# Banded attention before an MLP: from 128-row tiles turned by TensorE to 32x32 blocks turned by VectorE

## The chip, the cores and the metric

The kernel runs on one core of one Trainium2 chip. The metric is the device time of one execution in microseconds, and lower is better. Before the change three runs gave 407.55 us as the median, with 404.62 and 410.42 us as the ends.

## The reference

Eight batches of eight heads, 576 positions, head width 64. A query sees the keys within 32 positions on either side; eight global positions see everything and are seen by all. The attention result goes, token by token, through a two-layer MLP with softplus.

```python
scores = scale * np.matmul(q, k.transpose(0, 1, 3, 2))          # q, k, v: 8 x 8 x 576 x 64
mask = np.abs(pos[:, None] - pos[None, :]) <= window            # window = 32
mask = mask | is_global[:, None] | is_global[None, :]           # 8 global positions
scores = np.where(mask, scores, -1000000000.0)
attn = np.exp(scores - np.max(scores, axis=-1, keepdims=True))
attn = attn / (np.sum(attn, axis=-1, keepdims=True) + 1e-09)
x = np.matmul(attn, v) ...                                       # 4608 tokens x 512
h = x @ w_in                                                     # 512 -> 2048
g = np.maximum(h, 0.0) + np.log1p(np.exp(-np.abs(h)))
return g @ w_out                                                 # 2048 -> 512
```

## The kernel before

**The MLP.** The 4608 tokens are cut into nine tiles of 512. For each tile `first` (L770) makes 16 chunks of 128 hidden features with four matmuls each, `soft` (L776) applies softplus on ScalarE, and `second` (L781) makes four blocks of 128 tokens with 16 matmuls each, accumulated in one bank. `oev` copies a finished block out of PSUM and SyncE's queue writes it to memory. The first tile's `first` is done in two halves of 256 columns. Per tile this is 64 + 64 matmuls over 512 columns, in all kernels of this document.

**The attention of one unit.** A unit is 64 query positions of one batch, all eight heads, taken as four pairs of heads; there are 72 units, eight to a tile. `sc` (L632): for each pair of heads one matmul with the queries of both heads as 128 stationary columns (the query tile `qx` holds zeros in the other head's half) against 136 key columns: 128 positions around the unit and the eight global keys, which are stored among the others. `top` (L638), on VectorE, adds the mask and keeps the row extreme. `ex` (L659), on ScalarE, four exponentials with the row's own bias. `su` (L667 to L669): row sums and reciprocals on VectorE. `no` and `gc` (L675, L679), on GpSimd, multiply by the reciprocal. `tp` (L685): four 128x128 transposes by matmul, and `pt` copies them back from PSUM. `val` (L728, L735) takes four units: value matmuls over 64 columns, two column halves of the array at a time. The global queries' own rows are handled once a batch (`sg`, `mx`, `gexp`, `gsum`, `tg`, `lge`, `ov`, `oze`) and are laid into the result by a further small matmul group (`rt`, L728).

**The preparation of one batch.** GpSimd's queue loads q and k and casts them to bf16 on the way (`load_qk`, L233) into one buffer each, `qn` and `kn`. As there is one buffer, the load of the next batch waits until the transposes of this one are done. `pick` (L474) takes the global rows out by 64 small matmuls; `tk` and `tq` (L516, L524) turn k and q with 128 transposes by matmul, and `kev` and `qev` copy them out of PSUM. v is loaded by SyncE's queue, cast by GpSimd (L446), and copied a second time shifted by 64 rows (`shift`, two DMAs).

**What sets the order.** Each piece of work is a job with a cost written by hand for each engine that may do it. `_Order.run` lays all jobs out in time before the program is emitted and so fixes the order on every engine's queue and which engine does the copies. An engine works through its queue in that order: a job that is late holds up everything behind it. `KINDS` says how many of the eight PSUM banks a kind of job may hold, and `SLOTS` how many buffers there are. `gate` makes the exponentials of one tile wait until the softplus of the tile before is through, so that ScalarE changes its table twice a tile. `AHEAD` says how many units of the next tile are done early.

Of the kernel before, what the change touches and what calls it, by code (L numbers as in the profile page):

```python
# [18 lines left out]
class _Order:  # L19
# [17 lines left out]
    def add(self, cost, emit, deps=(), rank=5, opens=(), uses=(), table=None, moves=0, array=128):  # L37

        job = dict(cost=cost, emit=emit, deps=[d for d in deps if d is not None], rank=rank, opens=list(opens),
                   table=table, moves=moves, array=array, n=len(self.jobs), at=None, end=None)  # L40
# [13 lines left out]
    def room(self, opens):  # L54
# [3 lines left out]
        spare = 0  # L58
        for pool, key in opens:
            cap = self.slots.get(pool) or self.kinds[pool][0]  # L60
# [16 lines left out]
    def run(self, free):  # L77
# [13 lines left out]
        while ready:  # L91
            best = None
            for j in ready:
# [3 lines left out]
                if j["opens"]:  # L97
                    t = self.room(j["opens"])
                    if t is None:
                        continue  # L100
                    t0 = max(t0, t)
                for e in j["cost"]:
# [51 lines left out]
def kernel(  # L154
# [20 lines left out]
    G = 64  # L175
    NJ = S // G
    NT5 = (S + P - 1) // P
    NH5 = 2 * NT5
    HP = H // 2
    W = G + NG  # L180
    EXT = P + NG
    KD = d_model // P
    KF = d_ff // P
    NN = B * NJ
    NU = NN // 4
    assert d_model == H * D and D == 64 and S == 576 and NG == 8 and H == 8 and n_tokens == NN * G
# [6 lines left out]
    SUMMED = 9  # L193
    HALVED = 1
    W_IN = 1
    W_OUT = 4
    QK1 = 2
    AHEAD = [1, 2, 3, 3, 3, 3, 3, 3]

    TILES = [2] * (NU // 2)  # L200
    assert sum(TILES) == NU

# [3 lines left out]
    sets = ctx.enter_context(tc.tile_pool(name="setup", bufs=1))  # L206
# [4 lines left out]
    def temp(shape, dt, name):  # L211
        return sets.tile(shape, dt, tag=name, name=name)


    SRC = (q, k, v)
    QR = 8
    NQ = S // QR
    stage = ctx.enter_context(tc.tile_pool(name="stage", bufs=NT5))
    PS = {}

    def load_v(b, t):
        st = PS["in", b, 2, t] = stage.tile([P, H * D], FP32, tag="v", name="v")
        lo, hi = max(0, t * P - WIN), min(S, (t + 1) * P - WIN)
        p0 = lo - (t * P - WIN)
        nc.sync.dma_start(out=st[p0:p0 + hi - lo, :].rearrange("p (h d) -> p h d", h=H),
                          in_=SRC[2][b, :, lo:hi, :].rearrange("h s d -> s h d"))


    qn = const([P, H, QR * D], BF16, "qn")
    kn = const([P, H, QR * D], BF16, "kn")  # L230

    def load_qk(b, which, h0=0, h1=H):
        nc.gpsimd.dma_start(out=(qn, kn)[which][0:NQ, h0:h1, :],  # L233
                            in_=SRC[which][b, h0:h1].rearrange("h (q r) d -> q h (r d)", r=QR))

    load_qk(0, 1, 0, H // 2)
    vA = [const([P, NT5, H * D], BF16, f"vA{i}") for i in range(2)]
    vB = [const([P, NT5 - 1, H * D], BF16, f"vB{i}") for i in range(2)]

    gi = const([P, 2 * NG], I32, "gi")  # L240
    nc.sync.dma_start(out=gi[:, :], in_=global_idx.rearrange("(one n) -> one n", one=1).bitcast(I32)
                      .to_broadcast([P, 2 * NG]))

    load_qk(0, 0, 0, H // 2)
    ident = temp([P, P], FP32, "ident")
    make_identity(nc, ident[:])
    ident_b = const([P, P], BF16, "ident_b")
    nc.vector.tensor_copy(ident_b[:], ident[:])
# [4 lines left out]
    def clear(eng, ap):  # L253
        names = "abcd"[:len(ap.shape) - 1]
        flat = ap.rearrange("p " + " ".join(names) + " -> p (" + " ".join(names) + ")") if len(names) > 1 else ap
        eng.memset(flat.bitcast(I32), 0)

    gf = const([P, NG], FP32, "gf")
    nc.vector.tensor_copy(gf[:], gi[:, 0:2 * NG:2])
    posA = temp([P, NT5], FP32, "posA")  # L260
# [23 lines left out]
    def blank_q(i, eng):  # L284
# [3 lines left out]
        for p in range(HP):  # L288
            for h in range(2):
                eng.memset(qx[i][h * D:(h + 1) * D, p, :, 1 - h, :].bitcast(I32), 0)  # L290
# [658 lines left out]
```

## Time and profile before

| what | us |
|---|---|
| runs: lowest, median, highest | 404.62, 407.55, 410.42 |
| span of the profiled execution | 409.3 |
| VectorE, ScalarE, GpSimd busy in it | 247.2, 293.2, 149.8 |
| first MLP matmul starts | 38.56 |
| last piece of the chain, a copy of the last block, starts | 405.64 |

A row of the profile names the line, the engine, what is written and read, the count, the busy time, and the mean length of one instruction. The lengths of matmuls overlap, so the pace of a series is read from the starts in the timeline, not from the mean. "PEclk" is the clock granted to TensorE, 1.00 being full.

### The profile page before, as it was taken

To read this page: it belongs to the slowest core of one execution; us is meant where nothing else is said; L and a number is where in the kernel's file an instruction comes from. 1 tells how busy PE (TensorE), PEld (TensorE's weight loads), DVE (VectorE), ACT (ScalarE), POOL (GpSimd) and SP (SyncE) were. 2 spreads that over 40 slices of the span, in tenths; PEclk is the share of its full clock that TensorE was granted. 3 is DMA by queue.
4 is the path that set the end of the run, shared out by engine and by line. 5 is a ranking of instruction groups with operands and counts; after the bars stand their busy time and mean duration, and the time that the engine had idled before them with its cause. 6 is when DMAs were issued, how large, how long until landed. Compare 5 with 4: busy or idle time off the path is not lost.

```text
span 409.3 us, 11475 instructions
## 1 busy us (share of the span) xinstructions
PE 364.0 (89%) x4401; PEld 213.6 (52%) x4448; DVE 247.2 (60%) x1084; ACT 293.2 (72%) x736; POOL 149.8 (37%) x268
## 2 busy tenths in 40 slices
PE   2747999987999769998999799977999999999996
PEld 2525885653556345654565445634465455545442
DVE  5598758994598515874597429852587577334011
ACT  4486979884799628984898459951998698694720
POOL 8988133760078001840184005800183045023000
PEclk9999999999999969999999979996999999999999
DMA  6699968788021940159116911294012011001012
GB/s 97 138 194 198 202 136 163 171 183 129 0 74 41 179 99 27 54 97 188 55 54 98 176 38 51 46 193 101 27 54 80 0 54 54 0 27 53 0 54 77
DMA packets 61031, 37.47 MB, mean 92 GB/s; under 512 B 42032, under 2 KB 55344, under 8 KB 60976
## 3 DMA queue, kind: packets, MB, share of 16 engines
q0 software_dynamic: 16800, 13.65, 22.7%
q1 hardware_dynamic: 44176, 23.08, 21.7%
q8 instruction: 35, 0.57, 0.6%
q14 instruction: 20, 0.16, 0.1%
HBM read 36.71 MB, written 9.44 MB: 113 GB/s over the span
## 4 chain that ended last, share of the span: by engine, by line
PE 56%; DMA 18%; DVE 9%; POOL 8%; issue 4%; ACT 4%; POOLq 0%; DVEq 0%; ACTq 0%
PE o L781 23%; PE h L770 19%; DMA qn<-in_q_dram 18%; PE tp L685 3%; PE pick L474 2%; PE s L632 2%; DVE sm L667 2%; DVE st L638 2%; POOL vA L446 2%; DVE rs L669 2%; ACT pe L659 1%; PE xo L728 1%; POOL qx L290 1%; POOL pn L675 1%; PE xo L735 1%
## 5 line engine op out<-in xcount | busy, mean ns | idle before, releaser
L675 POOL TENSOR_TENSOR pn<-pe,rs 128x512 bf16<-128x512 f32 x72 | 74.9, 1041 | 202.9 <-DVE rs L669 191.5
L770 PE MATMUL h<-xT,win 128*128 128x512 bf16 (+1 forms) x620 | 141.8, 368 | 1.7 <-issue 0.7
L781 PE MATMUL o<-wout,g 128*128 128x512 bf16 x549 | 132.4, 379 | 1.5 <-issue 0.6
L776 ACT ACTIVATE g<-h 128x512 bf16<-128x512 f32 (+1 forms) x160 | 85.5, 558 | 47.8 <-PE h L770 45.2
L638 DVE CUSTOM_DVE_ANT_0 st<-s,mask 128x136 f32<-128x136 f32 x288 | 69.8, 296 | 55.5 <-PE s L632 52.8
L659 ACT ACTIVATE pe<-st,nb 128x136 f32<-128x136 f32 x288 | 93.9, 408 | 3.2 <-DVE nb L638 3.2
L770 PEld LDWEIGHTS <-win 128*128 128x128 bf16 x640 | 60.7, 100 | 50.3 <-issue 5.4
L781 PEld LDWEIGHTS <-g 128*128 128x128 bf16 x576 | 53.2, 98 | 51.4
L667 DVE TENSOR_REDUCE sm<-pe 128x4 f32<-128x544 f32 x63 | 44.9, 713 | 9.1 <-ACT pe L659 8.8
L685 PE MATMUL tp<-ident_b,pn 128*128 128x128 bf16 x288 | 28.9, 229 | 8.7 <-POOL pn L675 5.9
L632 PE MATMUL s<-kx,qx 128*128 128x136 bf16 x288 | 34.0, 239 | 0.3 <-issue 0.2
L632 PEld LDWEIGHTS <-qx 128*128 128x128 bf16 x288 | 24.6, 105 | 17.4 <-issue 4.6
L446 POOL CAST vA<-v 128x512 bf16<-128x512 f32 (+3 forms) x48 | 28.4, 611 | 13.4 <-DMA v<-in_v_dram 12.2
L685 PEld LDWEIGHTS <-pn 128*128 128x128 bf16 x288 | 19.9, 101 | 21.5 <-POOL pn L675 16.9
L419 ACT COPY qx<-tq 64x576 bf16<-64x576 bf16 x42 | 26.8, 637 | 4.5 <-PE tq L524 3.9
L419 DVE COPY osb<-o 128x512 f32<-128x512 f32 x18 | 12.4, 687 | 28.6 <-PE o L781 28.6
L638 DVE DVE_READ_ACCUMULATOR2_ANT nb<- 128x1 f32 x288 | 24.0, 83 | 0.0
L419 ACT COPY pt<-tp 128x512 bf16<-128x512 bf16 x34 | 19.9, 586 | 4.0 <-PE tp L685 3.8
L669 DVE TENSOR_SCALAR rs<-rs,notg 128x4 f32<-128x4 f32 x72 | 20.1, 280 | 2.7 <-DVE rs L668 0.2
L516 PE MATMUL tk<-ident_b,kn 72*64 72x72 bf16 x512 | 14.5, 206 | 8.2 <-DMA kn<-in_k_dram 8.2
L474 PE MATMUL pick<-qn,pick 72*32 72x128 bf16 x256 | 6.7, 265 | 16.7 <-DMA qn<-in_q_dram 16.4
L419 DVE COPY qx<-tq 64x576 bf16<-64x576 bf16 x22 | 16.6, 752 | 6.6 <-PE tq L524 6.4
(110 smaller groups left out, 423.0 us busy)
## 6 DMA issues: line engine op xcount, KB each, us to landing
out_dram<-osb SPq DMA_DIRECT2D x36, 256.0 KB, 2.0
v<-in_v_dram SPq DMA_DIRECT2D x24, 256.0 KB, 7.9
vB<-vA SPq DMA_DIRECT2D x16, 256.0 KB, 3.7
kn<-in_k_dram POOLq DMA_DIRECT2D x7, 576.0 KB, 9.7
qn<-in_q_dram POOLq DMA_DIRECT2D x7, 576.0 KB, 14.4
v<-in_v_dram SPq DMA_DIRECT2D x16, 192.0 KB, 4.6
win<-in_moe_w_in_dram POOLq DMA_DIRECT2D x4, 512.0 KB, 10.8
wout<-in_moe_w_out_dram POOLq DMA_DIRECT2D x4, 512.0 KB, 11.5
```

The costliest lines, as they stand in the source:

```text
L419: (nc.scalar.copy if e == "ACT" else nc.vector.tensor_copy)(out, in_)
L446: nc.gpsimd.tensor_copy(to[r], at[r])
L632: nc.tensor.matmul(out=ps[:, y, :], lhsT=qx[i][:, x * 2 + y, j, :, :].rearrange("c h q -> c (h q)"), rhs=kf[:, x * 2 + y, j * W:j * W + EX ...
L638: nc.vector.tensor_tensor_reduce(out=PS["st", n][:, p, :], in0=PS["s", n, x][:, y, :], in1=mask[:, j, :], scale=-SCALE, scalar=3.0e38, op0 ...
L659: nc.scalar.activation(out=pe[:, p, 0:EXT], in_=PS["st", n][:, p, :], func=AF.Exp, bias=PS["nb", n][:, p:p + 1], scale=-1.0, **({"accum_ou ...
L667: nc.vector.reduce_sum(out=sm[:], in_=PS["pe", n][:, :, 0:EXT], axis=AX)
L669: nc.vector.tensor_scalar(out=rs[:], in0=rs[:], scalar1=notg[:, j:j + 1], scalar2=None, op0=OP.mult)
L675: nc.gpsimd.tensor_tensor(out=pn[:].rearrange("c p (a s) -> c p a s", a=2), in0=wide[:, :, :, 0:G], in1=rs[:].unsqueeze(2).unsqueeze(3).to ...
L685: nc.tensor.transpose(out=ps[:, p, :], in_=PS["pn", n][:, p, :], identity=ident_b[:])
L770: nc.tensor.matmul(out=h[:, :], lhsT=w_in_t[c // 4][:, kd, c % 4 * P:(c % 4 + 1) * P], rhs=PS["xT", m][:, kd, lo:hi], start=(kd == 0), sto ...
L776: nc.scalar.activation(out=PS["g", m, c][:, lo:hi], in_=PS[key][:, :], func=AF.Softplus)
L781: nc.tensor.matmul(out=PS["o", m, ns][:, :], lhsT=PS["g", m, kf][:, ns * P:(ns + 1) * P], rhs=w_out_t[kf // 4][:, kf % 4, :], start=(kf == ...
```

## The change

The attention is rewritten; the MLP and the scheduler's principle stay. A "pair" n is now 128 query positions (four blocks of 32), all eight heads, so there are 36, four to a tile. The four quarters of the partitions hold heads: quarter r holds heads 2r and 2r+1, with the head width split in two halves (`w`) of 32.

- **Loads.** SyncE's queue loads q, k and v in fp32 into three staging buffers (for the first batch ScalarE's queue shares q and k). `add_cast` casts them to bf16 on GpSimd or ScalarE, two halves each; q and k are stored so that two neighbouring positions form a 4-byte pair. The load of the next batch waits for this cast only. The shifted copy of v is gone.
- **Turning.** `turn` transposes 32x32 blocks of such 4-byte pairs on VectorE, from SBUF to SBUF. The global key rows are written as one block of 32 columns between the others (`fill`), so a block's scores are four neighbouring blocks: previous, own, next, global.
- **Scores.** `sc`: for each block, half and head one matmul of a 32x32 tile over 128 columns, 64 in all for a pair; the two heads of a quarter go to different column quarters. For the first four pairs the mask is added by 32 more matmuls against an identity, and the exponentials are as before. For the others VectorE adds the mask (`ma`), takes the maximum over 1024 columns (`mx`), GpSimd subtracts it (`sub`), ScalarE does one exponential over 1024 columns (`ex`), VectorE sums (`su`), GpSimd multiplies and writes bf16 pairs (`no`), and VectorE turns them (`tp`).
- **Values.** `val` takes the four pairs of a tile (two in the first tile) in one job: for each two blocks four or five steps of eight matmuls on 32x64 tiles over 32 or 64 columns, which write four banks at once. The job is marked `urgent`: while it could start but lacks banks, the scheduler places nothing else that opens one. `vg` holds the finished rows of the global queries' own results in the place of the global block of values, so no separate group lays them in.
- **Global rows.** `sg` holds four banks; 48 matmuls. `mx`, `gexp`, `tpg` (a turn on VectorE), `ov` (144 matmuls on 32-row tiles over 64 columns), `gv`. `pick` has 72 matmuls for q and 72 for k, each over 128 columns.
- **Scheduler.** `KINDS` no longer asks for spare banks, `AHEAD` is one pair from the third tile on, and `room` counts several openings of one pool by one job.

```diff
-    KINDS = dict(h=(3, 1), o=(2, 1), s=(2, 1), pick=(1, 2), gt=(1, 1), tk=(2, 2), tq=(2, 2), sg=(2, 1), tg=(1, 0), ov=(1, 0),
-                 tp=(3, 0), rt=(1, 0), xo=(2, 0))
+    KINDS = dict(h=(3, 0), o=(2, 0), s=(4, 0), pick=(1, 0), sg=(4, 0), ov=(1, 0), xo=(4, 0))
...
+            first = []
+            for j in ready:
+                if j["urgent"]:
+                    t = self.room(j["opens"])
+                    first.append((j, max(d["end"] + self.HOP for d in j["deps"]), 1e9 if t is None else t))
...
+                    if any(pool in self.kinds for pool, key in j["opens"]) and any(
+                            u is not j and due <= t0 < free_at for u, due, free_at in first):
+                        continue
...
+    def load_qk(eng, b, w, rs):
+        for r in rs:
+            eng.dma_start(out=stage[w][quad(r), :, :, :].rearrange("i c e d -> i c (e d)"),
+                          in_=SRC[w][b, 2 * r:2 * r + 2].rearrange("h (c i e) d -> i (h c) (e d)", i=BL, e=2))
...
+        def turn(e, w):
+            if w == 0:
+                x = qb[:].rearrange("p c d e -> p c (d e)").bitcast(I32).rearrange("p (h c) (w i) -> p h c w i", h=2, w=2)
+                y = qx[i][:].bitcast(I32).rearrange("p h w (c i) -> p h c w i", i=BL)
+                V.transpose(out=y, in_=x)
+                return
...
+        def pck(e, w):
...
+            for c in range(NC):
+                for x in range(2):
+                    for r in range(R):
+                        nc.tensor.matmul(out=ps[quad(r), :, :], lhsT=pick[quad(r), c, x, g0:g0 + BL],
+                                         rhs=(qb, kb)[w][quad(r), :, :, x].rearrange("p (h c) d -> p h c d", h=2)[:, :, c, :],
+                                         start=(c == 0 and x == 0), stop=(c == NC - 1 and x == 1))
...
+            for x, (b, j) in enumerate(bl):
+                e0 = first_slot(j)
+                for w in range(2 + masked):
                     for h in range(2):
+                        for r in range(R):
+                            nc.tensor.matmul(out=PS["s", n, h][quad(col_of(r, h)), x, :],
+                                             lhsT=qx[b % 2][quad(r), h, w, j * BL:(j + 1) * BL] if w < 2 else eye[quad(r), :],
+                                             rhs=kx[b % 2][quad(r), h, w, e0 * BL:(e0 + SL) * BL] if w < 2 else
+                                             mask[quad(r), j, :, :].rearrange("p s i -> p (s i)"),
+                                             start=(w == 0), stop=(w == 1 + masked))
+
+        def ma(e, h):
+            V.tensor_tensor(out=PS["st", n][:, h, :, :], in0=PS["s", n, h][:, :, :],
+                            in1=mask[:, j0:j0 + PB, :, :].rearrange("p j s i -> p j (s i)"), op=OP.add)
...
+            V.reduce_max(out=m[:], in_=PS["s", n, h0][:] if masked else flat(PS["st", n], h0, h1), axis=AX)
...
+            nc.gpsimd.tensor_tensor(out=t, in0=t, in1=over(PS["m", n, y][:], SL * BL), op=OP.subtract)
...
+                nc.scalar.activation(out=t, in_=t, func=AF.Exp, scale=SCALE)
...
+                V.reduce_sum(out=sm[:], in_=flat(PS["st", n], h0, h1), axis=AX)
...
+            V.transpose(out=f[0], in_=f[1])
...
+                    steps = [(None, 0, 2, GLOB[a], GLOB[z])]
+                    if j > 0:
+                        steps.append((j - 1, 0, 1, PREV[a], None))
+                    steps.append((j, 0, 2, SELF[a], PREV[z]))
+                    steps.append((j + 1, 0, 2, NEXT[a], SELF[z]))
+                    if j + 2 < NJ:
+                        steps.append((j + 2, 1, 1, NEXT[z], None))
+                    for t, (key, x0, nx, s0, s1) in enumerate(steps):
+                        for h in range(2):
+                            for c in range(R):
+                                r = col_of(c, h)
+                                nc.tensor.matmul(
+                                    out=PS["xo", v_, r][h * D:(h + 1) * D, c0 + x0 * BL:c0 + (x0 + nx) * BL],
+                                    lhsT=vg[i][quad(c), h, :] if key is None else vb[i][quad(c), h, key, :],
+                                    rhs=near_by(n, c, h, x + x0, s0, s1),
+                                    start=(t == 0), stop=(t == len(steps) - 1))
```

## The prediction

> **What bounds the kernel now.** I read the busy shares first, then the spans in stretches of about one tile, then the chain of waits and the timeline of TensorE. The shares:
>
> ```profile
> PE 364.0 (89%) x4401; PEld 213.6 (52%) x4448; DVE 247.2 (60%) x1084; ACT 293.2 (72%) x736; POOL 149.8 (37%) x268
> ```
>
> TensorE leads, but a share says nothing of a stage. The stretches (span, busy time and count for PE, PEld, DVE, ACT, POOL, then granted clock, DMA share, GB/s) do:
>
> ```profile
> 80.00:120.00 40.00, 35.55 (x452) 20.34 (x456) 28.31 (x129) 30.02 (x71) 13.54 (x22) 1.00 0.47 94
> 120.00:165.00 45.00, 38.95 (x492) 22.25 (x498) 25.38 (x112) 31.09 (x76) 12.41 (x21) 0.92 0.43 84
> ...
> 300.00:345.00 45.00, 44.63 (x536) 25.23 (x542) 32.27 (x132) 38.16 (x94) 18.74 (x32) 1.00 0.13 43
> 345.00:390.00 45.00, 44.63 (x313) 22.82 (x316) 14.30 (x62) 32.02 (x63) 6.19 (x10) 1.00 0.07 24
> ```
>
> Late on, where nothing is loaded, TensorE is busy for 44.63 of 45 us: it is the bound. Where batches are loaded it idles 4 to 6 us and the clock falls to 0.92. The chain says why, with the timeline at one such place:
>
> ```profile
> 131.10 15.02 DMA qn<-in_q_dram
> 146.17 1.90 PE pick L474 x64
> ...
> 354.22 6.04 PE h L770 x28
> ...
> 398.10 7.52 PE o L781 x34
> ```
>
> ```profile
> 101.85 0.63 PE L474 MATMUL pick<-qn,pick 72*32 72x128 bf16 x32 [2.69 <-DMA qn<-in_q_dram]
> 102.31 0.62 PE L474 MATMUL pick<-kn,pick 72*32 72x128 bf16 x32
> 102.86 0.29 PE L632 MATMUL s<-kx,qx 128*128 128x136 bf16 x2
> ...
> 251.71 0.20 PE L735 MATMUL xo<-pt,vA 128*64 128x64 bf16 x2
> 251.74 0.20 PE L735 MATMUL xo<-pt,vB 128*64 128x64 bf16 x2
> 251.87 0.84 PE L685 MATMUL tp<-ident_b,pn 128*128 128x128 bf16 x8
> ```
>
> `pick` stands in TensorE's queue behind a q load of 15 us; the same 64 matmuls take 1.01 us (101.85 to 102.86) after a short wait, 1.90 us after a long one. The waits list puts 16.4 us on this load. Idle time of all stretches from 37 to 390 us adds to 22.8 us.
>
> Split of the time after the first MLP matmul: 405.6 − 38.6 = 367 us. The MLP is 1088 matmuls of 512 columns at 0.216 us (6.04/28) = 235 and 128 of 256 columns at half of that = 14, in all 249. Idle is 23. So 95 us are attention on TensorE, changes of its tile form among them.
>
> **TensorE after the change, in pieces.** Counted from the diff: scores 36·64 + 4·32 = 2432 matmuls over 128 columns; values 43 steps × 8 × 8 batches = 2752 over mostly 64; `pick` 1152 over 128; `sg` 384 over 288 in the mean; `ov` 1152 over 64. Together 7872, against some 3200 now.
>
> What one costs is the open question, since no row shows 32-row tiles. `pick` runs four column tiles at once: 1.01 us / 64 = 15.8 ns each, 63 ns a group. The value rows run two at once: a group each 30 to 32 ns (251.71, 251.74). So a group of concurrent tiles takes its columns' time plus little, however many are in it.
> - If eight tiles run at once in scores, `sg` and values (two heads in each of four quarters) and four in `pick` and `ov`: 2432/8 × 0.056 = 17, 2752/8 × 0.032 = 11, 1152 × 0.0158 = 18, 384/8 × 0.123 = 6, 1152/4 × 0.032 = 9. Sum 61 us.
> - If never more than four run at once, as `pick` shows: 38 + 22 + 18 + 12 + 9 = 99 us.
>
> I take 61: the tiles of a group share neither stationary place nor bank, and nothing in the rows shows a group growing with its members. The upper bound stays in the range. Moving operands with a step of two elements (`pick`, values) have no row either; if they halved the pace, values and `pick` would cost 29 us more.
>
> [...]
>
> Changes of tile form: from the last value group (251.74) to the next work is 0.13 us where groups follow each other every 0.03, so 0.1 us is lost. 78 groups of small tiles, most between 128-row work: 12 us.
>
> TensorE in all: 249 + 61 + 12 = 322, of which some 8 us (first batch's `pick`, `sg`, `ov`, first scores and values) lie before the first MLP matmul. 314 remain.
>
> **The loads.** q and k move from GpSimd's queue to SyncE's, and wait for a cast, not for TensorE. The next batch is asked for about a tile (36 us) ahead; a load took 15 us. So the 16.4 us of waits and the slow `pick` after them go; I charge nothing, since ahead of the load stands only a cast. SyncE's queue now has four q, four k and eight v issues a batch (five v issues took 6.80 us at 84.43), and the output writes queue behind them; an output block is due each 3.5 us and has two buffers, so an issue series of up to 7 us might cost about 2 us a batch. This is inside the stall term below. The shifted copy of v within SBUF (16 DMAs) disappears, off the path.
>
> **VectorE, per tile, by rows of before.** Mask add, 8 × 0.69 (the 128x512 cast out of PSUM took 689 ns) = 5.5; maximum and sum over 1024, each 713/544 × 1024 = 1.34 us, eight = 10.7, reciprocals 0.7; turns `tp`, for which no row exists: 512 words lie between 0.42 (bf16 copy of 512) and 0.69, I take 0.69, 2.8. Per batch: `turn` 2 × 1152 words at the same pace 2.7, `mxg` 2.4 (524 ns for 352 columns, 381 for 224), `tpg` 0.7, small ones 1.9: 7.7 × 8/9 = 6.8. Half the copies out of PSUM 2.8. Sum 29.3 us, against 247.2/9 = 27.5 now. If the turns ran at half pace, 5.5 us more.
>
> **The others, per tile.** ScalarE: exponentials fall from eight units of 1.63 us (408 ns × 4) to four of about 1.1, transposes' copies go, casts come: 25 us against 32.6. GpSimd: subtract and multiply at 2 × 1.04 = 2.08 us each, eight = 16.6, plus three of six casts at about 1.4: 21 against 16.6. All below TensorE's 314/9 = 35.
>
> **In order, does the exponential phase fit?** From the last softplus: table 1.3, `gexp` 2.8, first exponential 1.1, sum 1.5, three GpSimd multiplies 6.2, turn 0.7, values 1.4, copy 0.7: about 16 us. Beside it TensorE has 64 `second` matmuls (13.8 us), `sg`, `ov`, `pick`, later scores: 18 us. It fits, with little to spare.
>
> **Start and end.** Now the first scores start at 18.35 and the first MLP matmul at 38.56. After: k and q come 12 to 13 us after start, cast and turn 2.7, first scores near 16; two pairs' scores 1.7, sixteen exponentials of 0.39 = 6.3, `gexp` 3, multiply, turn, values (half clock) and copy 4: 31 us. The end (last copy and write) stays 3.7 us.
>
> **Stalls.** Idle without the load was 22.8 − 16.4 = 6.4 us over eight tiles; with a tighter phase I take double a tile, 9 × 1.7 = 15.
>
> Sum: 31 + 314 + 15 + 3.7 = 364 us against the profiled 409.3; the median of the runs is 1.75 us lower than that, so 362.
>
> **Rivals.**
> 1. *The queue cannot feed the small tiles.* If 15.8 ns a matmul, the least that any row shows, is a floor: 7872 × 0.0158 = 124, 63 more than the sum: 425 us. For: no row shows less. Against: both rows there are as fast as their columns allow, so neither shows the queue's own limit. Chance 0.15. [...]
> 2. *VectorE becomes the bound (the slower side).* A pair leaves VectorE after `mx` for `sub`, and after `su` for `no`, and VectorE's queue is fixed. If it stands through both multiplies of 2.08 us of each pair, a tile takes 29.3 + 16.6 = 46 us: 31 + 8 × 46 + 27.6 (last MLP) + 4 = 431. It decides once over 7 of those 16.6 us are uncovered, as a tile on TensorE takes 36.6 with stalls. For: VectorE now has steps before, between and after GpSimd's; for half-pace turns less is needed. Against: six score buffers let two pairs run ahead. Chance 0.20.
> 3. *Banks.* `sg` and `val` each want four of eight banks at once, 17 times, and while a due `val` waits nothing else opens one. One `second` block holds its bank 16 × 0.216 = 3.5 us; with 2.5 us lost each time: 362 + 43 = 405, no change. Chance 0.10.
>
> **How the numbers follow.** Forecast 0.55, the rivals 0.45. The likeliest case alone: 345 (no stalls, start at 29) to 399 (never more than four tiles at once, 38 more). The range must reach the rivals at 405, 425 and 431, and their uncertain sizes: 345 to 440, leaving out about 0.15. About 2% is what a measurement of this kernel can tell from no change, so faster is under 399, slower over 416: faster 0.55, same 0.10, slower 0.35.
>
> **What would show it.** The sum holds if no wait on a q or k load is left, first MLP work starts near 31 us, MLP matmuls keep 0.216 us, and scores take about 0.5 us a pair. Rival 1: scores of a pair take 1 us and values of a tile over 4. Rival 2: VectorE busy over 80% in the stretches with TensorE waiting on `tp`. Rival 3: gaps before `val` or `sg` ended by PSUM copies. Wrong altogether would be a GpSimd step far over 2.08 us: strided writes have no row here.

## The result and the profile after

The changed kernel takes 471.66 us as the median of four runs (466.70 to 473.27); the kernel before took 406.09 beside it (403.46 to 410.42). The ratio is 1.159, with a 95% interval from 1.149 to 1.168. The forecast of 362 us had the wrong sign, and its range ended at 440. The profiled execution has a span of 469.3 us. Ratios and their intervals, here and below, leave out the few slow executions of a kernel; medians are of all of them.

From the page after the change: the span, the busy shares, the granted clock in 40 slices, the queue that brings instructions (packets, MB, share), and the chain that ended last.

```profile
span 469.3 us, 19736 instructions
...
PE 362.0 (77%) x9038; PEld 206.2 (44%) x9088; DVE 247.3 (53%) x448; ACT 220.7 (47%) x410; POOL 173.2 (37%) x136
...
PEclk9955559996899979995999799979978999998899
...
q8 instruction: 71, 1.16, 1.1%
...
PE 74%; issue 16%; SPq 5%; DMA 3%; POOL 1%; DVE 1%; ACT 0%; ACTq 0%; POOLq 0%
```

No other engine has become the bound: all are below TensorE's share, and VectorE, ScalarE and GpSimd together hold 2% of the chain. TensorE itself went from 89% to 77% busy in a longer span, so it stands more. "issue" in the chain, time in which the engine waited for nothing that the profile shows, is 16%. The waits for q loads, 18% of the chain before, are gone: DMA is 3% of it. The line of q8 counts 71 packets of instructions; the page of the kernel before has half as many:

```profile
q8 instruction: 35, 0.57, 0.6%
```

The weight loads, one for each matmul, rose in the same proportion, from 4448 to 9088.

The same stretches as before (busy time and count by engine, granted clock, DMA share, GB/s), and one of the start:

```profile
0.00:57.00 57.00, 17.87 (x945) 15.28 (x946) 32.84 (x88) 21.63 (x84) 24.73 (x51) 0.72 1.14 200
80.00:120.00 40.00, 30.65 (x892) 20.80 (x896) 24.67 (x45) 24.24 (x42) 18.36 (x11) 0.87 0.64 139
120.00:165.00 45.00, 39.75 (x1311) 23.47 (x1324) 31.46 (x55) 24.14 (x38) 24.34 (x14) 0.99 0.65 143
300.00:345.00 45.00, 36.93 (x873) 19.87 (x878) 25.12 (x43) 20.36 (x34) 15.85 (x9) 0.89 0.19 52
345.00:390.00 45.00, 39.68 (x821) 20.32 (x826) 24.52 (x42) 20.35 (x34) 16.30 (x9) 0.92 0.07 26
```

From 300 to 390 us, where hardly anything is loaded and TensorE was busy for 44.63 of 45 us before, it now stands for 5 to 8 us in each stretch, at a clock of 0.89 to 0.92. The waits (engine, line, what was waited for: total, times, longest) say that it waits for "issue", most of all ahead of the small tiles, and ahead of MLP matmuls (L806) that come after such a series:

```profile
PEld L770 <- issue: 32.6, 20, 4.7
...
PE xo L770 <- issue: 28.0, 12, 4.6
...
PEld L622 <- issue: 24.8, 29, 4.2
...
PE s L622 <- issue: 19.1, 13, 4.0
...
POOL vb L414 <- DMA stage<-in_v_dram: 16.2, 1, 16.2
...
PE o L806 <- issue: 11.4, 22, 3.2
```

The timeline of TensorE at one tile's values shows the form of these stops (start, length, instructions of a row; in brackets the idle time ahead of it):

```profile
299.57 3.83 PE L806 MATMUL o<-wout,g 128*128 128x512 bf16 x17 [1.81 <-issue]
303.32 0.24 PE L770 MATMUL xo<-pt,vg 32*64 32x64 bf16 x8
303.38 0.44 PE L770 MATMUL xo<-pt,vb 32*64 32x32 bf16 x32
303.63 0.27 PE L770 MATMUL xo<-pt,vg 32*64 32x64 bf16 x8
...
305.26 0.25 PE L770 MATMUL xo<-pt,vb 32*64 32x32 bf16 x7
307.81 0.37 PE L770 MATMUL xo<-pt,vb 32*64 32x32 bf16 x25 [2.31 <-issue]
307.98 0.28 PE L770 MATMUL xo<-pt,vg 32*64 32x64 bf16 x8
308.08 0.49 PE L770 MATMUL xo<-pt,vb 32*64 32x32 bf16 x32
308.50 1.05 PE L622 MATMUL s<-kx,qx 32*32 32x128 bf16 x63
311.82 0.26 PE L622 MATMUL s<-kx,qx 32*32 32x128 bf16 x1 [2.27 <-issue]
```

TensorE stops in the middle of a series: seven of 32 equal matmuls run, then nothing for 2.31 us, then the other 25; the profile shows no operand that they wait for. Between the two stops stand 25 + 8 + 32 + 63 = 128 matmuls, each with its weight load: 256 instructions. A packet on q8 has 16 KB (1.16 MB in 71). All 9088 weight loads are in the trace. Counted through by 128, the first matmul behind a stop of over 0.7 us that ended on "issue" has a load with a number from 91 to 96, in 34 of 35 stops: nearly all lie at the same place modulo 256.

The packets themselves are in the trace's DMA records. The next table is worked out from them, for some stops: when TensorE stood, when the packet of the next block started and how long it took, from the packet's start to the first instruction, from the beginning of the block before to the packet's start, and the busy share of the DMA engines in the 4 us ahead of the packet (over 1: packets overlap in an engine).

```
stood             packet         to first   after block   DMA busy
                  start + took   instr.     began         before
25.62 -  30.75    28.15 + 0.92   2.60       4.14          1.22
32.91 -  37.22    34.31 + 1.33   2.91       3.56          1.22
45.81 -  50.04    47.70 + 0.95   2.34       4.12          1.20
110.92 - 113.56   111.03 + 1.06  2.53       1.20          0.66
213.45 - 216.59   214.25 + 0.97  2.34       2.21          0.70
252.59 - 254.11   251.51 + 1.28  2.60       1.13          0.01
309.24 - 311.82   309.33 + 1.16  2.49       1.51          0.51
431.15 - 433.86   431.30 + 1.19  2.57       1.18          0.00
```

So this is how it went in this execution. In 16 stops the block before began behind a stop itself, so that its beginning is seen exactly. In each of them the packet for the next block started only after the present block had been entered: 1.1 to 1.2 us later with idle DMA engines (busy share below 0.3, six stops), 1.2 to 2.2 us at shares of 0.5 to 0.7 (four), and 3.2 to 4.1 us later in five of the six with full ones (shares of 1.10 to 1.24; 1.9 in the other). The packet takes about 1 us (0.9 to 1.3 in the table), and its first instruction runs 2.2 to 2.9 us after its start, once 3.4. Such blocks come 3.4 to 3.7 us apart with idle DMA engines, in the start 6.4 to 6.7 (24.0 to 50.0 us). An MLP matmul takes 0.216 us, so a block of them lasts 27.6 us, longer than any of these distances; a block of small tiles at 8 ns lasts 1.0 us, and TensorE stands for the rest. No supply further ahead than one block shows in these stops.

The long stops also lower the granted clock (experiment 8, which fills those within the values, has it at 0.50 for 32.0 us behind the first MLP matmul, for 76.4 here). In the clock records of this execution, which begin at 21.2 us, it is 1.00 or 0.50. In the start it is 0.50 for 44.4 us (24.6 to 68.9). Later, but for the last one at the end, each stretch at 0.50 begins within or less than 1 us behind a stop of over 2 us, and is 3.4, 6.8 or 10.2 us long (for instance 307.9 to 314.7, behind the stop that ended at 307.81). Not every such stop is followed by one: 384.76 to 387.23 us is not.

Where the time went, by the starts of TensorE's matmuls: the time from one start to the next is booked on the first of the two, or as standing where it is over 0.7 us (us; "with filling" is an experiment below; standing ahead of the first MLP matmul is in the first row).

| | before | after | doubled | halved | joined (6) | with filling |
|---|---|---|---|---|---|---|
| up to the first MLP matmul | 38.6 | 57.0 | 69.9 | 53.7 | 53.3 | 62.2 |
| MLP matmuls | 252.0 | 259.5 | 269.8 | 261.6 | 254.3 | 252.0 |
| other matmuls | 92.5 | 84.1 | 113.5 | 61.2 | 82.7 | 87.5 |
| filling | | | | | | 42.9 |
| standing over 0.7 us | 22.1 | 64.5 | 110.0 | 39.2 | 52.2 | 38.6 |
| from the last matmul's start to the end | 4.1 | 4.3 | 4.3 | 4.2 | 4.3 | 4.2 |
| span | 409.3 | 469.3 | 567.4 | 420.0 | 446.8 | 487.4 |

The 60.0 us between the two kernels are 42.4 of standing, 18.4 of a later start and 7.5 of MLP, mostly at half clock, less 8.4 that the attention gained. Of the 64.5 us of standing, 62.9 in 29 of 31 stops ended on "issue"; of the 22.1 before, 2.5 did, and 17.6 ended with a q load. Behind the first MLP matmul the clock is at 0.50 for 76.4 us, before for 23.9.

### The profile page after: what moved, and what is told of

Its sections match the earlier page's. It is cut to its first block, busy times and chain, and to the rows that moved or that the text cites. A ratio compares the mean times of both kernels' runs of the same rounds, so it can differ in the third digit from the quotient of the medians.

```text
span 469.3 us, 19736 instructions
## 1 busy us (share of the span) xinstructions
PE 362.0 (77%) x9038; PEld 206.2 (44%) x9088; DVE 247.3 (53%) x448; ACT 220.7 (47%) x410; POOL 173.2 (37%) x136
## 3 DMA queue, kind: packets, MB, share of 16 engines
q8 instruction: 71, 1.16, 1.1%
## 4 chain that ended last, share of the span: by engine, by line
PE 74%; issue 16%; SPq 5%; DMA 3%; POOL 1%; DVE 1%; ACT 0%; ACTq 0%; POOLq 0%
PE o L806 28%; PE h L795 27%; PE xo L770 6%; PE s L622 5%; PE pick L495 4%; DMA stage<-in_k_dram 3%; PE ov L585 3%; SPq L241 2%; SPq L246 2%; PE sg L548 1%; POOL kb L414 1%; DVE xT L414 0%; ACT kb L414 0%; ACT g L801 0%; DVE osb L414 0%
## 5 line engine op out<-in xcount | busy, mean ns | idle before, releaser
L806 PE MATMUL o<-wout,g 128*128 128x512 bf16 x544 | 133.5, 398 | 11.9 <-issue 11.4
L676 POOL TENSOR_TENSOR pn<-st,rs 128x1024 bf16<-128x1024 f32 (+1 forms) x40 | 69.4, 1743 | 131.9 <-DVE rs L669 120.0
L806 PEld LDWEIGHTS <-g 128*128 128x128 bf16 x576 | 56.3, 101 | 80.7 <-issue 22.8
L647 POOL TENSOR_TENSOR st<-st,m 128x1024 f32<-128x1024 f32 x32 | 60.5, 1896 | 81.5 <-DVE m L639 81.5
L629 DVE TENSOR_TENSOR st<-s,mask 128x512 f32<-128x512 f32 x64 | 41.8, 675 | 11.5 <-PE s L622 11.3
L622 PE MATMUL s<-kx,qx 32*32 32x128 bf16 x2304 | 33.9, 248 | 15.6 <-issue 15.1
L667 DVE TENSOR_REDUCE sm<-st 128x8 f32<-128x1024 f32 x32 | 38.2, 1193 | 13.6 <-ACT st L660 13.6
L770 PE MATMUL xo<-pt,vb 32*64 32x64 bf16 (+1 forms) x2176 | 26.7, 210 | 23.5 <-issue 23.5
L639 DVE TENSOR_REDUCE m<-st 128x8 f32<-128x1024 f32 x32 | 38.6, 1206 | 0.2
L622 PEld LDWEIGHTS <-qx 32*32 32x32 bf16 x2304 | 26.2, 98 | 20.9 <-issue 20.6
L770 PEld LDWEIGHTS <-vb 32*64 32x64 bf16 x2176 | 24.4, 110 | 24.7 <-issue 24.5
L495 PEld LDWEIGHTS <-pick 32*32 32x32 bf16 x1152 | 20.2, 101 | 30.1 <-issue 11.8
L660 ACT ACTIVATE st<-st 128x1024 f32<-128x1024 f32 x32 | 32.1, 1054 | 0.1
L686 DVE STREAM_TRANSPOSE pt<-pn 128x512 int32<-128x512 int32 (+1 forms) x40 | 25.5, 639 | 5.0 <-POOL pn L676 5.0
L414 ACT COPY osb<-o 128x512 f32<-128x512 f32 x11 | 6.4, 582 | 45.7 <-PE o L806 27.6
```

What stands on the lines that cost most here:

```text
L414: {"ACT": nc.scalar.copy, "DVE": V.tensor_copy, "POOL": nc.gpsimd.tensor_copy}[e](out, in_)
L495: nc.tensor.matmul(out=ps[quad(r), :, :], lhsT=pick[quad(r), c, x, g0:g0 + BL], rhs=(qb, kb)[w][quad(r), :, :, x].rearrange("p (h c) d -> ...
L622: nc.tensor.matmul(out=PS["s", n, h][quad(col_of(r, h)), x, :], lhsT=qx[b % 2][quad(r), h, w, j * BL:(j + 1) * BL] if w < 2 else eye[quad( ...
L629: V.tensor_tensor(out=PS["st", n][:, h, :, :], in0=PS["s", n, h][:, :, :], in1=mask[:, j0:j0 + PB, :, :].rearrange("p j s i -> p j (s i)") ...
L639: V.reduce_max(out=m[:], in_=PS["s", n, h0][:] if masked else flat(PS["st", n], h0, h1), axis=AX)
L647: nc.gpsimd.tensor_tensor(out=t, in0=t, in1=over(PS["m", n, y][:], SL * BL), op=OP.subtract)
```

## The experiments

The theory: TensorE's instructions come in blocks of 256, and a stretch that uses one up faster than the next can come stands still. The rivals: small tiles cost their columns and the stops belong to other engines; each small matmul has a floor; the loads or the late v set the start. All kernels here are the changed one with the edit shown, or kernel 6 with it where that is said.

**1. More instructions, same columns.** Besides the scores below, the two-block steps of `val` and the steps of `ov` behind the first are cut in two in the same way.

```diff
-                            nc.tensor.matmul(out=PS["s", n, h][quad(col_of(r, h)), x, :],
...
+                            for z in range(1 + (w == 1)):
+                                zn = SL * BL // (1 + (w == 1))
+                                zs = slice(z * zn, (z + 1) * zn)
+                                nc.tensor.matmul(out=PS["s", n, h][quad(col_of(r, h)), x, zs],
...
```

> The same result and the same columns in the same order, with 3392 matmuls more: the second half of d in the scores goes as two matmuls of 64 columns, the two-block steps of the values as two of 32, the sums over V of the global rows as two of 32. Theory (instructions come to TensorE in blocks of 256, and a block takes about 3.4 us to come): 6784 instructions more are 26.5 blocks more, most of them inside bursts; worked out from the order of the instructions with 3.4 us a block, the pauses grow by 65 us, so 530 to 565 us, pauses still every 256 instructions, 97 instruction packets for 71. Rival A (a small tile costs its columns, the pauses belong to waits on other engines): 471 to 478 us. Rival B (a floor for each small matmul, 15 ns or so, eight tiles at once): 3392 x 15 ns = 51 us, about 520, but with no pauses at multiples of 256.

Measured 569.62 us, ratio to before 1.403 (1.386 to 1.421). The page of this kernel, queue and chain:

```profile
q8 instruction: 97, 1.59, 1.2%
...
PE 71%; issue 25%; DVE 3%; POOL 0%; DVEq 0%; POOLq 0%
```

The same sums cost 98 us more, 4.6 us above the theory's range. Standing behind the first MLP matmul grew by 45 us, and 54 of the 56 stops that ended on "issue" lie at the same place modulo 256 (loads 91 to 96 of 128) though there are now 97 blocks. That excludes rival A. A price per matmul, which the theory had not charged, exists too (29 us more in "other matmuls", 8.7 ns for each added one), but rival B's, with no stops, had 520 us.

**2. Fewer instructions.** The loops are those of `sc`, `pck` and `ov`.

```diff
-                for w in range(2 + masked):
+                for w in (0, 1, 2)[:2 + masked] if masked else (0,):
...
-                for x in range(2):
+                for x in range(1):
...
-                for m in range(NJ):
+                for m in range(0, NJ, 2):
```

> Leaves out half of the sums: the second half of d in the scores (but for the first four pairs), every second position of the gather of the global rows, every second key block of the global rows' values; 2304 matmuls less, all else in the same order. Theory (blocks of 256 instructions at about 3.4 us): 18 blocks less; pauses fall by 27 us and the matmuls' own time by about 18: 412 to 435 us, with a higher granted clock. Rival A (columns alone, pauses belong to other engines): 2304 matmuls at 8 ns, about 18 us, so 450 to 456. If VectorE, GpSimd or ScalarE set the pace: under 5 us gained.

Measured 418.83 us, 1.032 (1.014 to 1.049): within the theory's 412 to 435, far from the 450 to 456 of the columns. Standing fell by 25 us with 17 packets fewer.

**3. Later loads.**

```diff
-                add_load(b, w, T["cast", b - 1, w])
+                add_load(b, w, T["cast", b - 1, w] + ([T["val", 0]] if b == 1 else []))
...
-                                      [T["w_in", 3], T.get(("w_out", a - 1))], rank=4, moves=3100)
+                                      [T["w_in", 3], T.get(("w_out", a - 1)), T["val", 0]], rank=4, moves=3100)
```

> The loads of q and k of the second batch and of the second weight matrix are held until the first values have been issued, so that the DMA engines are nearly free while the first scores run. Theory with the addition that a block of instructions takes 5 to 6.5 us to come because it shares the DMA engines with 205 GB/s of loads: the start-to-start time of blocks before 57 us falls from 6.4 us to 4 or less, v lands before 31.9 us, the first MLP matmul starts at 43 to 50 us for 57, and the time is 8 to 15 us shorter (457 to 464). Rival (a block takes its time whatever else is loaded, or the start is set by VectorE and ScalarE): first MLP matmul within 3 us of 57, time 468 to 475, or longer where the late loads are missed afterwards.

Measured 481.76 us, 1.184 (1.171 to 1.197): slower than the change. The first MLP matmul came at 52.8 us, not at 43 to 50, and the loads were missed afterwards: standing behind it is 75.3 us for 64.5. The expectation's premise failed, for v and the first weights kept the DMA engines full up to 52 us by themselves (busy 1.2, with one dip to 0.9). Later in the same run four stops in a row show the dependence, though not strictly: the packet started 3.11 us after the block before began at a DMA share of 1.19, then 1.73 at 1.21, 1.05 at 0.29 and 1.10 at 0.00.

**4. The same matmuls, spread.** `pick`, `ov` and `val` are cut into pieces of 24 to 40 matmuls (the expectation's 40 to 48 is wrong), and the planner holds a piece back until its block can be there.

```diff
+    BLOCK = 256
+
+    def supply(self, j, step, t):
+        n = self.used + j["ins"]
+        k = n // self.BLOCK
+        if k == self.used // self.BLOCK:
+            return t, self.block
+        into = step * (self.BLOCK - self.used % self.BLOCK) / j["ins"]
+        long = 3400 if t > 45000 else 6000
+        new = max(t + into, self.block + long)
+        return new - into, new
```

> The same matmuls in another order. The pick, the global rows' sums over V and the values are cut into pieces of 40 to 48 matmuls, and the planner counts instructions: a piece that needs the next block of 256 is not placed earlier than 3.4 us after the block before it (6 us in the first 45 us), so that MLP matmuls are placed between. Theory: pauses worked out from the order fall by 11 us (75 to 64), because the MLP runs out of ready matmuls in the exponential phase; 445 to 465 us. Rival (pauses belong to small tiles or to other engines' waits): no gain, and the extra changes between tile forms and later xo evictions cost up to 15 us: 470 to 486.

Measured 491.40 us, 1.213 (1.200 to 1.226): a miss. From the first MLP matmul to the end it took 408.0 us for 412.3, with standing 60.5 for 64.5, so this spreading gains little; that few MLP matmuls are ready to stand between while the exponentials run is the likely reason, not shown. The loss is in the start (first MLP matmul at 79.0 us), where a cut `pick` of the second batch came to stand ahead of the first values and waited for its load (TensorE's timeline):

```profile
39.65 0.61 PE L516 MATMUL pick<-kb,pick 32*32 32x128 bf16 x16 [13.62 <-POOL kb L433]
```

**5 and 6. The same sums in fewer, wider matmuls.** The one-hot tiles of the four quarters (5), and then also the turned global probabilities (6), are put on the diagonal of a tile that is zero elsewhere.

```diff
-                    for r in range(R):
-                        nc.tensor.matmul(out=ps[quad(r), :, :], lhsT=pick[quad(r), c, x, g0:g0 + BL], ...
+                    nc.tensor.matmul(out=ps[:, :, :], lhsT=pick[:, c, x, g0:g0 + R * BL], ...
...
-                    for c in range(R):
-                        nc.tensor.matmul(out=ps[quad(c), h, :], lhsT=pgt[quad(c), h, m // 2, :, m % 2], ...
+                    nc.tensor.matmul(out=ps[:, h, :], lhsT=pgt[:, h, m // 2, :, :, m % 2].rearrange("p r i -> p (r i)"), ...
```

> The gather of the global rows with four 32x32 matmuls joined to one 128x128 matmul: the one-hot tile of each quarter is put on the diagonal of a tile that is zero elsewhere, so the sums, the columns and the 128-column passes are the same and 864 matmuls (1728 instructions, 6.75 blocks) are gone; nothing is left out. Theory (blocks of 256 instructions): 2 to 2.7 us a block (the steady part of the doubled and halved kernels gave 2.8 to 3.7 with their columns), so 13 to 18 us less: 453 to 458 us; first MLP matmul about 6 us earlier, since 216 of the instructions stand before it. Rival (columns set the price of small tiles): 466 to 473.

> As the kernel with the joined gather, and the global rows' sums over V joined in the same way: 864 matmuls less again (57 blocks in all for 71), for four VectorE transposes of a quarter each in place of one (2.0 us more a batch, on the way from the global exponential to these sums) and 36 passes of 64 columns in place of 144 small tiles four at a time. Theory: another 6.75 blocks, 13 to 18 us, less up to 8 us for the transposes in the chain: 440 to 452 us. Rival (columns): no gain from fewer instructions, and the transposes cost up to 16 us: 468 to 485.

Measured 459.54 us, 1.130 (1.118 to 1.142), and 448.93 us, 1.103 (1.093 to 1.113). The second lies inside its range, the first 1.5 us outside and far from the 466 to 473 of the columns. The sums and their columns are unchanged and nothing is left out. The tiles are wider, and (6) has three more turns a batch on VectorE; the count of instructions fell to 64 and 57 packets, and 12 and 23 us went. What I had wrong: the first MLP matmul came only 0.5 us earlier in (5). And "other matmuls" hardly fell (82.7 for 84.1 in (6)): the wide passes took about what four times as many small ones did; the gain of (6) is in standing (12.3 us), start (3.6) and the MLP's clock (5).

**7. Wider scores as well.** On kernel 6: two quarters of q on the diagonal, 64x64 tiles, at the price of turning q in eight instructions a batch.

```diff
-                V.transpose(out=y, in_=x)
+                for h in range(2):
+                    for r in range(R):
+                        V.transpose(out=y[quad(r), h, :, :, :, col_of(r, h) % 2, :], in_=x[quad(r), h])
```

> As the last one, and the scores on 64x64 tiles: two quarters of q stand on the diagonal of a tile that is zero elsewhere, 1216 matmuls less (48 blocks for 71); q is turned by eight VectorE transposes a batch in place of one (about 4.5 us more each batch), and four buffers of scores in place of six, for room. Theory: 23 blocks less at 2 to 2.7 us is 46 to 62 us, less 0 to 15 for VectorE: 407 to 440 us, granted clock above 0.92, issue below 10% of the chain. Rival A (columns): 468 to 490. Rival B (VectorE, now 300 us busy, becomes the bound): above 440, with idle TensorE ended by VectorE.

Measured 468.45 us, 1.151 (1.140 to 1.163): the theory's range missed. Rival B's is met, and by the time alone rival A's too (468 to 490). Only 48 packets are left and "issue" is 10% of the chain, but VectorE holds 34% of it, for 22% in kernel 6 (page, chain; then the row of the turns of q, and from the changed kernel that of a turn on all partitions: busy time, mean ns):

```profile
PE 48%; DVE 34%; issue 10%; DMA 4%; SPq 2%; ACT 1%; POOL 0%; DVEq 0%; ACTq 0%; POOLq 0%
```

```profile
L485 DVE STREAM_TRANSPOSE qx<-qb 32x576 int32<-32x576 int32 x64 | 49.1, 767 | 3.6 <-POOL qb L422 1.4 <-ACT qb L422 1.3
```

```profile
L577 DVE STREAM_TRANSPOSE pgt<-pg 128x576 int32<-128x576 int32 x8 | 5.9, 733 | 0.0
```

A turn of 576 words on 32 partitions takes 0.77 us; on all 128 partitions 576 words take 0.73 (`tpg`). Cutting by partitions saves nothing, so turning q costs 49 us for 10.9. Against kernel 6, standing behind the first MLP matmul fell from 52.2 to 46.7 us, other matmuls took 91.1 for 82.7, and the first MLP matmul came at 66.4 for 53.3: most of the loss lies in the start, where TensorE's queue has scores of the second batch, which wait for its q load and its turns, ahead of the first values. How much of it is VectorE's is not shown.

**8. Useless work in the stops.**

```diff
+                    rem = 512 - c0 - 2 * BL
+                    for z in range(min(6, -(-1800 // rem)) if rem >= 128 else 0):
+                        nc.tensor.matmul(out=PS["xo", v_, z % R][:, 512 - rem:512], lhsT=w_in_t[0][:, 0, 0:P],
+                                         rhs=w_in_t[0][:, 0, 0:rem], start=True, stop=True)
```

> The changed kernel with matmuls of no use put into the values: after each stretch of 32 or 40 small ones, some 0.75 us of wide ones (up to six, over columns of the same banks that are not begun yet; later overwritten), so that TensorE works through the time in which it would stand for the next block of instructions; about 3.7 us of such work a tile, in the same order of jobs, 66 instructions more a tile. Theory (pauses come from the supply of instructions, and the granted clock falls to 0.5 behind them): the pauses within the values go, the time that they took is taken by the useless matmuls, and the clock keeps at 1.0 behind the values: 450 to 465 us, clock above 0.90. Rival (the clock falls with small tiles themselves, or the pauses are of another kind and stay): 33 us of work more, 485 to 505 us, clock 0.87 to 0.89.

Measured 489.18 us, 1.192 (1.182 to 1.202), the rival's size, with the theory's mechanism. (The values here also wait for the first part of `w_in`, whose tile the filling reads.) The clock of this run, and its timeline within the values:

```profile
core 0: 487.4 us, clock 0.968
```

```profile
173.40 0.44 PE L770 MATMUL xo<-pt,vb 32*64 32x32 bf16 x32
173.78 1.12 PE L777 MATMUL xo<-win 128*128 128x448 bf16 x5
174.83 0.23 PE L770 MATMUL xo<-pt,vg 32*64 32x64 bf16 x8
174.88 0.28 PE L770 MATMUL xo<-pt,vb 32*64 32x32 bf16 x24
```

Stops over 0.7 us within the values fall from 11 with 29.9 us to 4 with 8.0, standing falls by 26 us, the time at half clock behind the first MLP matmul from 76.4 to 32.0, and the MLP takes 252.0 us again, as in the kernel before. (The mean clocks, 0.886 and 0.968, do not compare: this trace has no clock record before 61.5 us, where the other has its 44.4 us at 0.50.) So the small tiles by themselves neither stop TensorE within the values nor lower the clock behind them. But the filling took 42.9 us, a mean of 0.15 us for each matmul, against the 26 + 7.5 that it saved, and the start came 5 us later.

**9 and 10. The start, and all together.** On kernel 6, q and k of the second batch are held until `no` of the second pair (9); then with the filling of 8 (10).

```diff
-                add_load(b, w, T["cast", b - 1, w])
+                add_load(b, w, T["cast", b - 1, w] + ([T["no", 1, 0]] if b == 1 else []))
```

> The kernel with joined gather and sums over V (448.9 us), and the loads of q and k of the second batch held until the second pair of the first tile is normalized, so that v of the first batch, w_in and TensorE's instructions have the DMA engines to themselves, and the casts and gathers of the second batch stand behind the first MLP matmuls. Theory: the blocks before the first MLP matmul come in 4 to 5 us for 6.3, it starts at 40 to 47 us for 53.3, and 5 to 12 us are left of it: 437 to 444 us. Rival (the loads are missed later, as with all of them held): 447 to 460.

> The last one with the useless matmuls within the values. If both theories hold, the gains add: 425 to 438 us; still slower than the kernel before (ratio 1.04 to 1.07), because some 30 us of pauses and the start stay. If the useless matmuls only cost: 455 to 475.

Measured 451.27 us, 1.099 (1.089 to 1.110), and 468.64, 1.145 (1.137 to 1.153): both theories missed, both times within the other range. The first MLP matmul of (9) came at 51.5 us, and up to then the DMA engines stayed full with what was left to load (stretch of the start):

```profile
40.00:53.00 13.00, 5.55 (x196) 4.61 (x197) 8.21 (x24) 7.44 (x30) 5.67 (x6) 0.50 1.23 209
```

**11 and 12. Weights later too.** Both weight matrices wait for the first tile's scores, q and k of the second batch for the first values; in the changed kernel (11) and in kernel 6 (12).

```diff
-        T["w_in", x] = o.add({"POOL": (780, 0)}, ..., [T["load", 0, 0], T.get(("w_in", x - 1))], ...
+        T["w_in", x] = o.add({"POOL": (780, 0)}, ..., [T["sc", 3], T.get(("w_in", x - 1))], ...
```

> The changed kernel with the loads of both weight matrices held until the first tile's scores have been issued, and q and k of the second batch until the first values: once v of the first batch has landed the DMA engines have nothing to move. The MLP then waits for its weights, so no gain in time is meant: 465 to 490 us. Theory (a block of instructions comes late in the start because it shares full DMA engines): from the landing of v on, blocks come 3.4 to 4.0 us apart for 6.4, their packets start within 2 us of the block before, and the first tile's last scores are done at 30 to 35 us for 38.4. Rival (blocks are slow in the start for another reason): still 6 to 6.7 us apart, last scores at 37 to 40.

> The same holding of loads in the kernel with joined gather and joined sums over V (448.9 us). Theory: as above for the blocks in the start; first values 3 to 8 us earlier, then a wait for w_in; 440 to 460 us. Rival: no block comes earlier, and the weights come later: 455 to 470.

Measured 471.57 us, 1.152 (1.141 to 1.163), and 451.96, 1.107 (1.099 to 1.115). The DMA engines were less full but not idle, and the blocks of the start came accordingly: in (11) 4.8 and 5.6 us apart for 6.4, with packets 2.3 and 2.8 us after their blocks at shares of 0.70 and 1.02. The 3.4 to 4.0 us of the theory were not reached, nor was the rival's 6 to 6.7 kept. The last scores of the first tile were done at 33.1 us for 38.8 in (11), the first values of (12) began at 42.9 for 48.2, both as the theory had it, and the first MLP matmul came at 49.3 and 48.1 us. This fits a start that depends on the load of the DMA engines, though a start with idle engines was not reached. In time (11) gained nothing and (12) lost 3 us: the later work lost it again.

No version beat the kernel before. The best are kernels 6 and 9, at 1.103 and 1.099 of it, which their intervals do not tell apart.

## Why the prediction was wrong

**The step that failed** is the charge for stalls, 15 us, and with it the start at 31. I took the idle time of the kernel before and doubled it, and never asked how fast TensorE's instructions come. The page of before had the line (35 packets on q8), and I counted 7872 small matmuls for 3200 without laying the one beside the other. The runs put 64.5 us of standing in that term's place, 62.9 of it on "issue", in 29 stops of which 28 lie where a block ends; the kernel before has 22.1 by the same count.

The prediction's sum, 363.7 us, is 105.6 short of the span of 469.3. Of this, 49.5 are stalls (64.5 for 15), 26.0 the start (57.0 for 31), 29.6 TensorE's work behind it (343.6 for 314: MLP 259.5 for 249, attention 84.1 for 65) and 0.6 the end.

In the start, missing instructions are not the only cause. The chain that ended last goes through most of it by another way (start, length, what):

```profile
19.04 6.94 SPq L241
...
30.09 7.08 DMA stage<-in_k_dram
...
40.28 1.03 PE pick L495 x30
```

From 7.7 to 30.1 us it runs through SyncE's queue, in which the issues of v and k loads stand one behind the other (the eight of v take 12.5 us). Then come a k load of the second batch, its cast, and its `pick`, which stands ahead of the first tile's `ov` in TensorE's queue; three stops of 9.3 us together follow. I had charged nothing for waits on loads. Holding q and k of the second batch back, with the second weight matrix, brought the first MLP matmul of the changed kernel from 57.0 to 52.8 us (3), and with both to 49.3 (11); in kernel 6 it came from 53.3 to 51.5 (9, without the weights) and 48.1 (12).

- **Start.** First scores at 19.1 us, for 16 predicted; then four blocks, each 6.4 to 6.7 us after the last. First MLP matmul at 57.0 for 31. TensorE waits 23.1 us of this on "issue". The wait of GpSimd for v, 16.2 us, lies in the same time; kernel 6, in which it was 0.4 us, still began its MLP at 53.3. How the 26 us divide between loads and instructions stays open.
- **Small tiles, 61 us.** Somewhat low at full clock, and by a partly wrong reason. 64 scores take 0.52 us (163.33 to 163.85 with filling), 40 value matmuls 0.31 us (303.32 to 303.63): 8 ns each, whether over 128, 64 or 32 columns. In the scores more than four tiles run at once, by an estimate from `pick`, which with four at once has 14.0 ns for each over the same 128 columns, and this though the four quarters of `s` write the same bank. That it is all eight is not shown, and no kind goes much below 8 ns a matmul; I had 7 for scores and 4 for values. Scores take 8.1 ns, values 8.2, `ov` 7.8, `pick` 14.0 and `sg` 14.6 (medians of uninterrupted series at full clock). By these paces all are 73 us: scores 20, values 23 for my 11, `pick` 16, `sg` 6, `ov` 9. In the run they took 99.6 (84.1 and 15.5 ahead of the MLP), the rest being half clock, changes of form and short stops.
- **Rival 1** named the mechanism, a queue that cannot feed the small tiles, but as a floor for each matmul of 15.8 ns. The least pace in these runs is half of that, about 8 ns; what costs is the block. Its 425 us were nearer by luck, and its signs did not come: a pair's scores take 0.52 us, not 1.
- **Rivals 2 and 3** did not happen: VectorE 53% busy, 70% at most in a stretch of 45 us (120 to 165); ahead of `sg` no stop, ahead of values one of 0.4 us (`vg`) and ahead of scores one of 0.5 us was ended by work that reads PSUM.
- **What held.** TensorE's waits for q and k loads are gone. An MLP matmul takes 0.216 us at full clock; the MLP's 7.5 us more are mostly half clock (30.4 us of its matmuls' time lie at 0.50, before 9.0). VectorE 247 us in all (29.3 a tile would be 264), ScalarE 24.5 a tile for 25, GpSimd 19.2 for 21, a turn of 512 words 0.69 as taken, strided writes of GpSimd 1.9 for 2.08. So three of the four signs that I named for the sum came true (no such wait, 0.216 us, about 0.5 us for a pair's scores), while the sum failed: none of them looks at stops within a series.
- **The attention's gain** behind the first MLP matmul was put at 95 − 65 = 30 us on TensorE (61 + 12, less 8 ahead of it). It came to 8.4.

## What to carry to other kernels

Count instructions per microsecond, not only columns: in this kernel a stretch that uses 256 TensorE instructions (128 matmuls with their weight loads) in less than about 3.5 us, or 6.4 us while loads fill the DMA engines, stops at the end of each block, and the clock often falls behind it. Signs of it on a page are "issue" ahead of the smallest matmuls, stops within a series, and the packets of the instruction queue; small matmuls of several quarters joined on a block diagonal cost the same passes and a quarter of the instructions (11 to 12 us by the ratios for each 864 saved here). Before changing to smaller tiles, compare the count of that queue with the time in which the bursts run.

## What the hardware showed unexpectedly

- Matmuls on 32-row tiles start about 8 ns apart at full clock, over 128 columns (scores, 8.1), 64 (`ov`, 7.8) or 32 and 64 (values, 8.2) alike.
- The packet with TensorE's next 256 instructions starts after the present ones are entered: 1.1 to 1.2 us later with idle DMA engines, mostly 3.2 to 4.1 with full ones; then it is 2.2 to 2.9 us to the first instruction.
- Turning 32x32 blocks on VectorE goes by words for each partition: 576 words take 0.77 us on 32 partitions and 0.73 on 128.
